# Gradient tiles loaded by GpSimd instead of SP, the first block's leaf C by halves of channels, and a newly planned order in the weight gradient

## Chip, cores and metric

One core of a Trainium2 chip runs one program. The metric is the device time of one execution in microseconds (us); 16 DMA engines serve the core. Engine names are those of the profile: PE (matrix multiplications; PEld its weight loads), DVE (elementwise work on vectors), ACT (activations and copies), POOL (GpSimd; here it clears buffers and issues DMAs), SP (issues DMAs). The memory on the chip is one buffer called arena; ps is the accumulator memory that PE writes.

## What is computed

A strided convolution (31 taps, stride 2, 256 channels to 256), a normalisation over time for each channel, a GELU, and the gradients of all inputs. Two sequences (batch) of 16000 steps, bfloat16:

```
h = sum over i < 31 of einsum('blc,cd->bld', x[:, i:i + 2*L:2], w[i])     # L = 7985
mu  = mean of h over l
var = mean of (h - mu)**2 over l
out = gelu((h - mu) / sqrt(var + 1e-5) * gamma + beta)
outputs: out, then the gradients for x, w, gamma and beta given grad_out
```

## The kernel before

The convolution and its two gradients are split three times in the manner of Karatsuba: two halves A and C_ and a combination B_, so that three products stand for four at each level, at the price of sums and differences on DVE. A bottom product is called a **leaf**. Where a leaf's weights or inputs can be differenced once more, it is computed by `f_three_b` and `f_three_ac` (f for the forward pass) instead of `f_leaf`: one product with a weight difference, three copies on ACT inside ps, and then the outer products onto the copies.

There are five stages. F0 and F1 are the forward pass of the two sequences (matmuls on line 742), G0 and G1 the gradient for x (line 1330), W the gradient for w (line 1537). W goes through nine combinations n = 0 to 8; each takes tiles of x from memory (`x_raw`, `x_more`, 1 MB and 512 KB), tiles of h's gradient (`d_tile`: for each of two sequences one load of 640 KB and one of 576 KB from the scratch memory dld), forms sums of x (lines 1502, 1603, 1607) and differences of d (`pair_d`, lines 1618 and 1623; `leaf_d`, lines 1703 and 1708) on DVE, and multiplies them on PE. The scratch memory dld is written during G0 and G1 by POOL (line 550).

No instruction's place is written by hand. A class `Plan` records each operation with its engine, an assumed duration and what it depends on (`add`); `order` works out when each is due, by going back from the matmuls that need it, and shifts the due time by two tables: `lead` (by the kind of operation) and `fine` (by kind and by n in W). `listing` then lets each engine take, among what is ready, the operation that is due first, and `emit` writes the program in the order that results. On each engine the program then runs strictly in that order. A load goes to SP, except that `load(..., "POOL", own=True)` lets POOL issue it. So a wait of SP for a buffer holds back every DMA behind it on SP; the same goes for POOL.

The start is `f_first` (line 966), the first block of F0. Four ps tiles are used; `pa`, `pc` and `pb` take the leaves A, C_ and B_. Weights are loaded slot by slot by SP (16 loads, most of 256 KB). DVE then makes the weight sums (`w_sub`, line 684): differences W[B][slot] and the second differences WD. DVE's sums of x are line 700; one of them, `third(C_, U[2])`, serves leaf C alone. Three pieces follow in time on PE: leaf A (channel half 0 in two pieces, then half 1), leaf C by `f_three_b` (16 matmuls of 256 columns) and `f_three_ac` (32 of 256), and leaf B in the same way. Line 837 (`keep`) is ACT's reading of leaf B's finished ps tile, the end of this block on PE.

Of the kernel before, what the change touches and what calls it, by code (L numbers as in the profile page):

```python
# [20 lines left out]
A, B_, C_ = 0, 1, 2  # L21
# [17 lines left out]
class Plan:  # L39
# [3 lines left out]
    def __init__(self, tc):  # L43
# [88 lines left out]
            "W keep w_keep": -3.0,  # L132
            "W keep weight_grad": -12.5,
            "W leaf_d weight_grad": 0.5,
            "W load d_tile": -54.0,
            "W load out0_late": 115.0,
            "W load w_done": -7.5,
            "W load w_emit": 28.0,
            "W load weight_grad": 2.0,
            "W load x_more": -9.0,  # L140
            "W load x_raw": 1.0,
            "W pair_d weight_grad": 1.5,
            "W pair_x weight_grad": 1.5,
            "W turn out0_late": -21.0,
            "W ve w_done": -11.0,
            "W ve weight_grad": -25.0,
            "W w_add weight_grad": 2.5,
            "W w_add x_more": 1.5,
            "W w_add x_tile": 29.5,
            "W w_both weight_grad": 11.0,  # L150
            "W w_emit w_done": 13.0,
            "W w_emit weight_grad": -261.0,
            "W w_mm w_leaf": -10.0,
            "W w_pairs weight_grad": -112.5,
        }
        self.spare = {k + " dl_turn": 3.0 for k in ("G0 turn", "G0 load", "G1 turn", "G1 load")}
        self.room, self.mixed = 2048.0, 2.2
# [80 lines left out]
            "W keep w_keep": {0: 2.5, 3: -11.5, 4: 11.0, 5: 6.5, 6: -13.0},  # L238
            "W keep weight_grad": {0: 7.0, 1: 1.5, 2: -4.0, 3: -2.0, 4: 23.5},
            "W leaf_d weight_grad": {0: 1.5, 1: -14.5, 2: -49.5, 3: 27.0, 4: -0.5, 5: -6.5, 6: -16.0, 7: 12.5, 8: -21.0},  # L240
            "W load d_tile": {0: 71.0, 1: 51.0, 2: 44.0, 3: 39.5, 4: 1.0, 5: 4.0, 6: -11.5, 7: 28.0, 8: 93.0},
            "W load out0_late": {0: -80.0, 8: 80.5},
            "W load w_emit": {5: -31.0, 6: -58.5, 7: -34.5, 8: 24.0},
            "W load weight_grad": {7: 81.5},
            "W load x_more": {2: -1.5, 4: 1.0, 5: -17.5},
            "W load x_raw": {0: -0.5, 2: -30.5, 4: 0.5, 5: -92.0, 6: -11.5, 7: 24.0},
            "W pair_d weight_grad": {0: -2.5, 1: -7.5, 2: -34.0, 3: -23.5, 4: 38.0, 5: -129.0, 6: -205.5, 7: -22.0, 8: 4.5},
            "W pair_x weight_grad": {0: 3.0, 1: -23.5, 2: 39.5, 3: -23.0, 4: -14.0, 5: 2.0, 6: -9.5, 7: 27.5, 8: -76.0},
            "W turn out0_late": {0: -66.0, 8: -137.0},
            "W ve w_done": {2: 12.0},  # L250
            "W ve weight_grad": {5: -21.5, 7: 12.0, 8: -47.0},
            "W w_add weight_grad": {0: 16.5, 1: -5.0, 2: 8.5, 3: -0.5, 4: -51.5, 5: -0.5, 6: -28.5, 7: -43.5, 8: 53.0},
            "W w_add x_more": {2: 20.0, 4: 2.0, 5: 34.0},
            "W w_add x_tile": {1: -101.0, 3: -75.5},
            "W w_both weight_grad": {0: -43.0, 1: -23.0, 3: -1.5, 6: -18.0, 7: -12.5, 8: 28.0},
            "W w_emit w_done": {5: -1.5, 6: 5.0, 7: -9.0, 8: -30.5},
            "W w_emit weight_grad": {8: 240.0},
            "W w_mm w_leaf": {2: -7.5, 3: -150.5, 4: 42.5, 5: -233.0, 6: 12.5, 8: 6.0},
            "W w_mm w_pairs": {0: -7.0, 1: 7.0, 2: -47.0, 3: -10.0, 4: -139.5, 5: 2.5, 6: -395.0, 7: 6.0, 8: 14.0},
            "W w_mm w_single": {0: 2.5, 1: 3.5, 2: -9.0, 3: -1.5, 4: -211.5, 5: -4.5, 6: -3.0, 7: 1.5, 8: -24.5},  # L260
            "W w_pairs weight_grad": {0: 25.5, 2: -11.5, 3: 41.5, 4: 15.5, 6: -37.0, 7: -5.0, 8: -17.0},
        }
        self.npe = 0
        self.stage, self.part = "F0", 0
# [206 lines left out]
def conv_stem_kernel(  # L471
# [15 lines left out]
    K, _, D = w.shape  # L487
    P = 128
# [3 lines left out]
    HM = 256  # L492
# [72 lines left out]
    W = {B_: sb(0, 3, 2, 4, 2, D), A: sb(24576, 3, 2, 4, 2, D), C_: sb(49152, 3, 2, 4, 2, D)}  # L565
# [4 lines left out]
    U = [sb(o, 2, F) for o in (138240, 142592, 205312)]  # L570
# [191 lines left out]
    def f_three_b(ps, br, lf, op, co, we):  # L762


        jobs = []
        for dh in range(2):
            for q2 in range(2):
                for par in range(2):
                    for ch in range(2):
                        o0 = (2 * par + ch) * XM + co + q2  # L770
                        n = we if q2 + par + ch else HM
                        jobs.append((0, slice(HM * dh, HM * dh + n), WD[br, lf][:, ch, q2, par, dh * P:(dh + 1) * P],
                                     op[:, 1, o0:o0 + n], dh + q2 + par + ch == 0))
        f_mm(ps, jobs, [ps[:, 0]], [WD[br, lf], op[:, 1]])
        for o, i, sc in ((ps[:, 1, 0:HM], ps[:, 0, HM:512], 1.0), (ps[:, 1, HM:512], ps[:, 0, HM:512], -1.0),
                         (ps[:, 0, HM:512], ps[:, 0, 0:HM], -1.0)):
            add("ACT", act(256), [o], [i],
                lambda o=o, i=i, sc=sc: nc.scalar.activation(out=o, in_=i, func=ACT.Copy, scale=sc))  # L778

    def f_three_ac(ps, br, lf, u, co, we, wo):  # L780
        for half, ua, ww in ((0, u[:, 0], we), (1, u[:, 1], wo)):
            for dh in range(2):
                jobs = []
                for q2 in range(2):
                    for par in range(2):
                        for ch in range(2):
                            q = 2 * q2 + half
                            if i_tap(q, par, br, lf) < K:
                                o0 = (2 * par + ch) * XM + co + q2
                                jobs.append((dh, slice(HM * half, HM * half + ww),  # L790
                                             W[br][:, lf, ch, q, par, dh * P:(dh + 1) * P], ua[:, o0:o0 + ww], False))
                f_mm(ps, jobs, [ps[:, dh]], [W[br][:, lf], ua, ps[:, dh]])
# [1073 lines left out]
```

## Time and profile before

| | |
|---|---|
| device time, median of 3 runs | 1148.43 us (1147.74 to 1150.5) |
| time of the profiled execution | 1148.4 us |
| its span (first to last instruction) | 1146.6 us |
| PE busy | 1117.3 us, 97% |
| DVE busy | 998.8 us, 87% |
| ACT busy | 532.4 us, 46% |
| POOL busy | 124.4 us, 11% |

A row of the timeline shows where a group starts (us from the span's start), how long it takes, its engine, line, operation and tiles, how many there are, and in brackets how long the engine was idle before the group and who ended that idle time ("<-DVE arena L684": a DVE instruction of line 684). A view of windows shows, for each stretch, what each engine was busy and (x) how many instructions it ran, then the granted clock of PE (1.00 is full speed), the mean share of the 16 DMA engines that was busy, and the rate in GB/s. Line numbers of the kernel after are larger by one in every function (742 becomes 743, and so on).

### The profile page before, as it was taken

What the parts mean: (1) busy time and instruction counts of PE and PEld (TensorE: products, weight loads), DVE (VectorE), ACT (ScalarE), POOL (GpSimd) and SP (SyncE); (2) the same over time, 40 slices, a digit from 0 to 9 for tenths busy, and PEclk for the clock granted to TensorE, in tenths of its full rate; (3) what the DMA queues carried; (4) which work ended last, traced back from release to release, by engine and by line L of the source; (5) the groups of instructions that cost most, each with busy time, mean ns of one, the idle gap of its engine ahead of it and who ended that gap; (6) DMA issues with size and microseconds to landing.
All of it is one profiled execution on the core that took longest, in us unless ns stands there. A gap on an engine that the chain in (4) does not pass through costs nothing. (4 is left out here: it accounts for less than half of the span.)

```text
span 1146.6 us, 18837 instructions
## 1 busy us (share of the span) xinstructions
PE 1117.3 (97%) x7598; PEld 749.3 (65%) x7652; DVE 998.8 (87%) x932; ACT 532.4 (46%) x817; POOL 124.4 (11%) x221
## 2 busy tenths in 40 slices
PE   5999999999999999999999899999999999999998
PEld 3888899877777884444444444444488766666785
DVE  7997787798989998998999777976799998788995
ACT  1254453768777488987744255633212212111200
POOL 0000000000000002231233133232200000000000
PEclk8999999999999999999999999999999999999999
DMA  9476658678895699999989688886998815999564
GB/s 220 66 175 138 164 139 172 147 189 192 193 222 132 192 363 277 280 259 277 229 224 218 136 214 190 205 214 163 247 334 267 291 64 200 350 333 308 185 199 128
DMA packets 345999, 243.57 MB, mean 212 GB/s; under 512 B 233569, under 2 KB 317159, under 8 KB 341735
## 3 DMA queue, kind: packets, MB, share of 16 engines
q1 hardware_dynamic: 338807, 223.47, 73.4%
q0 software_dynamic: 7104, 18.89, 5.8%
q8 instruction: 60, 0.98, 0.4%
q14 instruction: 28, 0.23, 0.1%
HBM read 106.24 MB, written 80.25 MB: 163 GB/s over the span
## 5 line engine op out<-in xcount | busy, mean ns | idle before, releaser
L742 PE MATMUL ps<-arena 128*128 128x256 bf16 (+4 forms) x3460 | 408.4, 282 | 12.6 <-DMA arena<-in_x_dram 6.0
L1330 PE MATMUL ps<-arena 128*128 128x512 bf16 (+1 forms) x1833 | 401.6, 377 | 9.5 <-DVE arena L1283 3.3
L742 PEld LDWEIGHTS <-arena 128*128 128x128 bf16 x3460 | 339.1, 99 | 81.7 <-DMA arena<-in_x_dram 6.3
L1330 PEld LDWEIGHTS <-arena 128*128 128x128 bf16 x1872 | 183.6, 98 | 226.3 <-issue 10.2
L1537 PE MATMUL ps<-arena 128*128 128x256 bf16 (+1 forms) x2305 | 308.3, 296 | 3.4 <-DVE arena L1703 1.8
L1537 PEld LDWEIGHTS <-arena 128*128 128x128 bf16 x2320 | 226.7, 98 | 85.1 <-DVE arena L1607 1.9
L837 ACT ACTIVATE arena<-ps 128x1024 f32<-128x1024 f32 x109 | 110.8, 1021 | 253.1 <-PE ps L1537 82.7
L700 DVE TENSOR_TENSOR arena<-arena 128x2080 bf16<-128x2080 bf16 (+8 forms) x126 | 156.5, 1266 | 34.4 <-PE ps L742 33.8
L550 POOL DMA_DIRECT2D dld<-arena x144 | 104.3, 727 | 259.7 <-DMA arena<-arena 247.3
L1117 DVE TENSOR_TENSOR arena<-arena 128x2048 bf16<-128x2048 bf16 (+1 forms) x80 | 95.6, 1195 | 9.1 <-ACT arena L1109 4.9
L1283 DVE TENSOR_TENSOR arena<-arena 128x1032 bf16<-128x1032 bf16 (+1 forms) x126 | 87.4, 725 | 8.1 <-ACT arena L1232 4.8
L1502 DVE TENSOR_TENSOR arena<-arena 128x4096 bf16<-128x4096 bf16 (+1 forms) x50 | 87.1, 1773 | 5.9 <-DMA arena<-in_x_dram 5.7
L1391 DVE TENSOR_TENSOR ps<-ps,arena 128x2048 f32<-128x2048 f32 x30 | 68.9, 2297 | 24.9 <-PE ps L1330 13.8
L1401 DVE TENSOR_TENSOR arena<-ps,arena 128x1024 bf16<-128x1024 f32 x64 | 77.0, 1218 | 8.0 <-PE ps L1330 5.3
L857 ACT ACTIVATE arena<-ps 128x512 bf16<-128x512 f32 (+1 forms) x64 | 37.1, 581 | 54.0 <-PE ps L742 53.5
L1639 ACT COPY ps<-ps 128x256 f32<-128x256 f32 x54 | 19.3, 358 | 84.2 <-PE ps L1537 82.5
L559 POOL MEMSET arena<- 128x128 bf16 (+11 forms) x40 | 8.6, 245 | 428.3 <-DVE arena L700 139.9
L1357 ACT COPY ps<-ps 128x512 f32<-128x512 f32 x48 | 27.7, 577 | 48.6 <-PE ps L1330 48.4
L1708 DVE TENSOR_TENSOR arena<-arena 128x4608 bf16<-128x4608 bf16 x16 | 40.6, 2551 | 4.7 <-PE ps L1537 4.7
L812 ACT ACTIVATE arena<-ps 128x512 f32<-128x512 f32 x56 | 29.6, 597 | 32.3 <-DVE ps L822 18.8
L778 ACT ACTIVATE ps<-ps 128x256 f32<-128x256 f32 x75 | 27.6, 369 | 35.3 <-PE ps L742 34.1
L1623 DVE TENSOR_TENSOR arena<-arena 128x2048 bf16<-128x2048 bf16 x36 | 42.8, 1219 | 1.4 <-PE ps L1537 1.4
(81 smaller groups left out, 716.5 us busy)
## 6 DMA issues: line engine op xcount, KB each, us to landing
arena<-in_x_dram SPq DMA_DIRECT2D x28, 1024.0 KB
dld<-arena POOLq DMA_DIRECT2D x144, 128.0 KB, 4.0
arena<-hd SPq DMA_DIRECT2D x32, 512.0 KB
out_dram<-arena SPq DMA_DIRECT2D x14, 1024.0 KB
arena<-in_x_dram SPq DMA_DIRECT2D x26, 512.0 KB
arena<-dld SPq DMA_DIRECT2D x18, 640.0 KB
arena<-dld SPq DMA_DIRECT2D x18, 576.0 KB
vl<-arena SPq DMA_DIRECT2D x36, 256.0 KB
```

What stands on the lines that cost most here:

```text
L550: lambda: e.dma_start(out=out, in_=in_), dma=np_ * ns / 16e3 * 1.03, ns=ns, tp=SH[pk], slack=slack)
L700: lambda: nc.vector.tensor_tensor(out=o, in0=a, in1=b, op=ALU.add))
L742: yield nc.tensor.matmul(ps[:, dh, cs], lhsT=wt, rhs=mv, start=s0, stop=False, skip_group_check=True)
L837: lambda: nc.scalar.activation(out=out, in_=ps, func=ACT.Copy, scale=scale))
L1117: add("DVE", dve(nf), [o], [a, b_], lambda: V.tensor_tensor(out=o, in0=a, in1=b_, op=op))
L1283: lambda: nc.vector.tensor_tensor(out=o, in0=a, in1=b, op=ALU.subtract))
L1330: yield nc.tensor.matmul(ps[:, e, 0:wide], lhsT=lt, rhs=mv, start=s0, stop=False, skip_group_check=True)
L1391: lambda: nc.vector.tensor_tensor(out=o, in0=x, in1=g, op=ALU.add))
L1401: lambda: nc.vector.tensor_tensor(out=ho[:, :, k, :], in0=ps[:], in1=g, op=ALU.add))
L1502: add("DVE", dve(o.free_size()), [o], [a, b], lambda: nc.vector.tensor_tensor(out=o, in0=a, in1=b, op=ALU.add))
L1537: yield nc.tensor.matmul(ps[:, s, c0:c1], lhsT=lt, rhs=mv, start=s0, stop=False, skip_group_check=True)
L1623: add("DVE", dve(2048), [o], [u, v], lambda o=o, u=u, v=v: nc.vector.tensor_tensor(out=o, in0=u, in1=v, op=ALU.subtract))
```

## The change

Three edits. The rows of the tables `lead` and `fine` for stage W get new numbers, so that the order of W is another one (a few of those rows are shown). In `f_first`, leaf C is computed by `f_leaf` in two pieces, by halves of channels, where it was `f_three_b` with `f_three_ac`; `third(C_, U[2])` goes. And `d_tile` loads from POOL's queue.

```diff
@@ tables of stage W (all its rows change)
-            "W load d_tile": -54.0,
+            "W load d_tile": -66.0,
-            "W pair_d weight_grad": 1.5,
+            "W pair_d weight_grad": -1.0,
...
-            "W pair_d weight_grad": {0: -2.5, 1: -7.5, 2: -34.0, 3: -23.5, 4: 38.0, 5: -129.0, 6: -205.5, 7: -22.0, 8: 4.5},
+            "W pair_d weight_grad": {0: -8.5, 1: -23.0, 2: -53.5, 3: -0.5, 4: 3.5, 5: -1.0, 6: -217.0, 7: 0.5, 8: 19.0},
@@ def f_first(xt)
-        third(C_, U[2])
         third(B_, U[1])
         pa, pc, pb = ring[0], ring[1], ring[3]
         f_leaf(pa, B_, A, ops[A], 0, HM, HM, True, (0,), (0,))
         f_leaf(pa, B_, A, ops[A], 0, HM, HM, False, (0,), (1,))
         f_leaf(pa, B_, A, ops[A], 0, HM, HM, False, (1,))
-        for ps, lf, u in ((pc, C_, U[2]), (pb, B_, U[1])):
-            f_three_b(ps, B_, lf, ops[lf], 0, HM)
-            f_three_ac(ps, B_, lf, u, 0, HM, HM)
+        f_leaf(pc, B_, C_, ops[C_], 0, HM, HM, True, (0,))
+        f_leaf(pc, B_, C_, ops[C_], 0, HM, HM, False, (1,))
+        f_three_b(pb, B_, B_, ops[B_], 0, HM)
+        f_three_ac(pb, B_, B_, U[1], 0, HM, HM)
@@ def d_tile(n, b)
             load(v.rearrange("p r d -> p (r d)"),
-                 bass.AP(tensor=t.tensor, offset=t.offset, ap=[[8 * D, P], [1, k * D]]), k * 65536, 4096)
+                 bass.AP(tensor=t.tensor, offset=t.offset, ap=[[8 * D, P], [1, k * D]]), k * 65536, 4096, "POOL", own=True)
```

What this does to the order is shown at three places. The names in brackets at a row's end are semaphores: DVE_49 counts DVE's finished instructions, DMAHW and DMASW those of DMAs issued by SP and by POOL. Between the first block and the end of G1 the order of PE, DVE and ACT is the same in both programs but for a weight difference that DVE makes later.

PE, at the end of the first half of leaf A (24 matmuls), before:

```order
L742 LDWEIGHTS arena
L742 MATMUL ps<-arena 128x256
L742 LDWEIGHTS arena [waits DVE_49]
L742 MATMUL ps<-arena 128x256 [waits Activation_49]
L742 LDWEIGHTS arena
L742 MATMUL ps<-arena 128x256
```

The same place now, and 48 rows (24 weight loads, 24 matmuls) further on:

```order
L743 LDWEIGHTS arena
L743 MATMUL ps<-arena 128x256
L743 LDWEIGHTS arena [waits DVE_49]
L743 MATMUL ps<-arena 128x512
L743 LDWEIGHTS arena
L743 MATMUL ps<-arena 128x512
```

```order
L743 LDWEIGHTS arena
L743 MATMUL ps<-arena 128x256
L743 LDWEIGHTS arena [waits DVE_49]
L743 MATMUL ps<-arena 128x512 [waits Activation_49]
L743 LDWEIGHTS arena
L743 MATMUL ps<-arena 128x512
```

Before, PE went from leaf A's first half to leaf C's 16 matmuls with the weight differences WD, DVE's sixth `w_sub` of the sixteen that follow on line 684; leaf A's second half came after them. Now leaf A's second half comes at once and waits for DVE's second `w_sub`; then comes leaf C, whose first half waits for the seventh, and leaf B's two pieces come last. On DVE the sixteen `w_sub` stand in another order to suit, with one sum of line 700 less ahead of them; on SP four loads of weights for leaf A's second half stand ahead of leaf C's eight, where they stood behind.

DVE, at the change from G1 (1391, 1401) to W, before:

```order
L1607 TENSOR_TENSOR arena<-arena 128x2048 [waits DVE_49]
L1401 TENSOR_TENSOR arena<-ps,arena 128x2x512 [waits DMAHW2_49,PE_49]
L1618 TENSOR_TENSOR arena<-arena 128x1024 [waits DMAHW7_49,PE_49]
L1618 TENSOR_TENSOR arena<-arena 128x1024 [waits DMAHW3_49]
L1401 TENSOR_TENSOR arena<-ps,arena 128x2x512
L1401 TENSOR_TENSOR arena<-ps,arena 128x2x512 [waits DVE_49,PE_49]
L1401 TENSOR_TENSOR arena<-ps,arena 128x2x512 [waits PE_49]
L1703 TENSOR_TENSOR arena<-arena 128x2304 [waits DMAHW4_49]
L1703 TENSOR_TENSOR arena<-arena 128x2304 [waits DMAHW5_49]
L1618 TENSOR_TENSOR arena<-arena 128x1024 x2
L1703 TENSOR_TENSOR arena<-arena 128x2304
L1623 TENSOR_TENSOR arena<-arena 128x2048 [waits DVE_49,PE_49]
```

and now:

```order
L1608 TENSOR_TENSOR arena<-arena 128x2048 [waits DVE_49]
L1402 TENSOR_TENSOR arena<-ps,arena 128x2x512 [waits DMAHW7_49,PE_49]
L1402 TENSOR_TENSOR arena<-ps,arena 128x2x512 [waits PE_49]
L1402 TENSOR_TENSOR arena<-ps,arena 128x2x512 [waits DVE_49,PE_49]
L1402 TENSOR_TENSOR arena<-ps,arena 128x2x512 [waits PE_49]
L1608 TENSOR_TENSOR arena<-arena 128x2048 [waits DVE_49] x2
L1619 TENSOR_TENSOR arena<-arena 128x1024 [waits DMASW3_49]
L1619 TENSOR_TENSOR arena<-arena 128x1024 [waits DMASW4_49]
L1619 TENSOR_TENSOR arena<-arena 128x1024 x2
L1704 TENSOR_TENSOR arena<-arena 128x2304 [waits DMASW5_49]
L1704 TENSOR_TENSOR arena<-arena 128x2304
```

The four small differences of `pair_d` (1618, now 1619) stand behind the four of line 1402 and behind two sums of x (1608); two of them stood between the former. On PE, the first 8 matmuls of W now stand behind the last of G1 (they stood ahead of its last 4); 24 more of W follow, and the next one needs the first 1619.

SP, in combination n = 1 and 2 of W, before, with the d tiles dld among the x tiles:

```order
L550 DMA arena<-in_x_dram 128x4x512
L550 DMA arena<-dld_1_81 128x2560
L550 DMA arena<-dld_1_90 128x2560
L550 DMA arena<-in_x_dram 128x4x512
L550 DMA arena<-dld_1_81 128x2304
L550 DMA arena<-dld_1_90 128x2304
L550 DMA arena<-in_x_dram 128x4x512
L550 DMA arena<-in_x_dram 128x8x512 x3
```

SP there now, and behind it POOL where its stores to dld end:

```order
L551 DMA out_dram<-arena 1024x1x256 x4
L551 DMA arena<-in_x_dram 128x4x512 x4
L551 DMA arena<-in_x_dram 128x8x512 x4
L551 DMA arena<-in_x_dram 128x4x512 x4
L551 DMA pcd_98<-arena 128x1024
```

```order
L551 DMA dld_4_93<-arena 128x2x256 x2
L551 DMA arena<-dld_0_80 128x2304
L551 DMA arena<-dld_0_89 128x2304
L551 DMA arena<-dld_0_80 128x2560
L551 DMA arena<-dld_0_89 128x2560
L551 DMA dld_7_96<-arena 128x2x256 x2
L551 DMA arena<-dld_2_82 128x2560
L551 DMA arena<-dld_2_91 128x2560
```

All 36 loads of d tiles have left SP; on POOL four of them stand ahead of the last two stores of dld, and the other 32 follow one another, with nothing but a small store behind them.

More of the change, by code (lines that the diff above doesn't have):

```diff
@@ L131, in __init__ @@
             "G1 zero e_comp": -8.0,
-            "W keep w_keep": -3.0,
-            "W keep weight_grad": -12.5,
-            "W leaf_d weight_grad": 0.5,
-            "W load d_tile": -54.0,
[L136 to L141, printed above, removed]
-            "W pair_d weight_grad": 1.5,
+            "W keep w_keep": -1.0,
+            "W keep weight_grad": -73.0,
+            "W leaf_d weight_grad": -5.5,
+            "W load d_tile": -66.0,
+            "W load out0_late": 45.0,
+            "W load w_done": -6.0,
+            "W load w_emit": 41.5,
+            "W load weight_grad": 97.5,
+            "W load x_more": -8.5,
+            "W load x_raw": 2.0,
+            "W pair_d weight_grad": -1.0,
             "W pair_x weight_grad": 1.5,
-            "W turn out0_late": -21.0,
-            "W ve w_done": -11.0,
-            "W ve weight_grad": -25.0,
+            "W turn out0_late": -103.0,
+            "W ve w_done": -7.0,
+            "W ve weight_grad": -18.0,
             "W w_add weight_grad": 2.5,
[L148 to L154, printed above, removed]
+            "W w_add x_tile": -39.0,
+            "W w_both weight_grad": 11.5,
+            "W w_emit w_done": 12.0,
+            "W w_emit weight_grad": -291.5,
+            "W w_mm w_leaf": -13.5,
+            "W w_mm w_pairs": -0.5,
+            "W w_pairs weight_grad": -125.0,
         }
@@ L237, in __init__ @@
             "G1 zero e_comp": {2: 20.0, 3: 23.0},
[L238 to L243, printed above, removed]
@@ new lines, in __init__ @@
+            "W keep weight_grad": {0: 14.0, 1: 68.0, 2: 4.0, 3: -18.0, 4: 3.5},
+            "W leaf_d weight_grad": {0: -10.5, 1: 24.5, 2: -54.0, 3: 14.5, 4: 20.5, 5: 27.0, 7: 33.5, 8: -21.0},
+            "W load d_tile": {0: 63.0, 1: 10.0, 2: 27.0, 3: 76.5, 4: -1.0, 5: -10.0, 6: 7.5, 7: -27.0, 8: 96.0},
+            "W load out0_late": {0: -50.0, 8: 220.5},
+            "W load w_done": {3: -0.5},
+            "W load w_emit": {5: -54.0, 6: -73.5, 7: -47.5, 8: 9.0},
+            "W load weight_grad": {7: -53.0},
@@ new lines, in __init__ @@
+            "W load x_more": {2: -9.5, 4: 2.0, 5: -17.5},
+            "W load x_raw": {0: -0.5, 2: -3.5, 4: -0.5, 5: -119.5, 6: -14.0, 7: 6.5},
+            "W pair_d weight_grad": {0: -8.5, 1: -23.0, 2: -53.5, 3: -0.5, 4: 3.5, 5: -1.0, 6: -217.0, 7: 0.5, 8: 19.0},
+            "W pair_x weight_grad": {0: 4.5, 1: 4.0, 2: 39.5, 3: -19.0, 4: -11.0, 5: -7.5, 6: -12.0, 7: 27.0, 8: -35.0},
+            "W turn out0_late": {8: -124.0},
+            "W ve w_done": {2: 10.5},
+            "W ve weight_grad": {5: 37.5, 6: -31.0, 7: 15.0, 8: -10.5},
@@ L262, in __init__ @@
+            "W w_mm w_pairs": {0: -8.5, 1: -223.0, 2: -142.5, 3: -5.0, 4: -227.5, 5: 10.0, 6: -259.0, 7: 6.0, 8: 14.0},
+            "W w_mm w_single": {0: 2.5, 1: 3.5, 2: -0.5, 3: -1.5, 4: -196.0, 5: -37.0, 6: -4.0, 7: 2.5, 8: -84.5},
+            "W w_pairs weight_grad": {0: 1.5, 1: 3.0, 2: -8.5, 3: -11.5, 4: 10.0, 5: 13.5, 6: -5.5, 7: -23.0, 8: -9.0},
         }
```

25 lines of the change are left out of this document (8 added, 17 removed).

## Prediction

> **What bounds the kernel.** I read the page first, then PE's timeline at the start and in W, then DVE's and ACT's beside it, and last the windows for the clock and the DMA engines.
>
> ```profile
> span 1146.6 us, 18837 instructions
> PE 1117.3 (97%) x7598; PEld 749.3 (65%) x7652; DVE 998.8 (87%) x932; ACT 532.4 (46%) x817; POOL 124.4 (11%) x221
> ```
>
> PE is busy for 1117.3 of 1146.6 us, so what can be won is the 29.3 us in which it is idle, and time in which its clock is low. The change touches two places: the first 40 us and the stage W, from about 825 us on. Here is PE at the start, then DVE and ACT.
>
> ```profile
> 12.21 6.44 PE L742 MATMUL ps<-arena 128*128 128x512 bf16 x24 [1.88 <-DVE arena L700]
> 23.07 37.15 PE L742 MATMUL ps<-arena 128*128 128x256 bf16 x307 [4.42 <-DVE arena L684]
> ...
> 12.67 3.53 DVE L700 TENSOR_TENSOR arena<-arena 128x2080 bf16<-128x2080 bf16 x3
> 16.12 18.24 DVE L684 TENSOR_TENSOR arena<-arena 128x2048 bf16<-128x2048 bf16 x16
> 34.28 2.33 DVE L700 TENSOR_TENSOR arena<-arena 128x4192 bf16<-128x4192 bf16 x1
> ...
> 33.64 1.17 ACT L778 ACTIVATE ps<-ps 128x256 f32<-128x256 f32 x3 [5.71 <-PE ps L742]
> 39.77 1.03 ACT L837 ACTIVATE arena<-ps 128x1024 f32<-128x1024 f32 x1 [4.96 <-PE ps L742]
> ```
>
> PE ends leaf A's first half at 12.21 + 6.44 = 18.65 and stands until 23.07. Leaf C's matmuls wait for the sixth of the sixteen weight differences: 16.12 + 6 x 1.14 (18.24 / 16) = 22.96. ACT's line 837 waits for PE and starts at 39.77, so the first block ends on PE at about 39.65. From 23.07 to 60.22 PE has no wait.
>
> ```profile
> 20.00:22.00 2.00, 0.00 (x0) 0.00 (x0) 2.00 (x3) 0.00 (x0) 0.00 (x0) 0.84 1.31 140
> 22.00:24.00 2.00, 0.93 (x5) 0.69 (x6) 2.00 (x2) 0.00 (x0) 0.00 (x0) 0.50 1.05 236
> ...
> 26.00:28.00 2.00, 2.00 (x10) 1.09 (x8) 2.00 (x3) 1.10 (x3) 0.00 (x0) 0.50 0.36 76
> 28.00:30.00 2.00, 2.00 (x17) 1.55 (x16) 2.00 (x3) 0.00 (x0) 0.00 (x0) 0.95 0.00 0
> ...
> 32.00:36.00 4.00, 4.00 (x35) 3.18 (x34) 4.00 (x4) 1.10 (x3) 0.00 (x0) 1.00 0.00 0
> 36.00:40.00 4.00, 4.00 (x39) 3.57 (x37) 4.00 (x5) 0.23 (x1) 0.00 (x0) 1.00 0.00 0
> ```
>
> The wait costs twice. The granted clock is 0.50 until about 28.2 (0.95 from 28 to 30 us is 0.2 us at half), so from 23.07 on some 5.13 us run at half speed: 10 matmuls in 2 us against 74 in 8 us at full clock, 0.108 us each. Half of 5.13, 2.56 us, is lost to the clock.
>
> **The start, step by step.** The times of the new order by these rows:
> - DVE has one sum of line 700 less (3.53 / 3, with overlap 1.15 us), so the sixteen differences start at 14.97. Leaf A's first half is untouched and ends at 18.65. Its second half needs the second difference, at 14.97 + 2.28 = 17.25, and runs on without a wait: 24 matmuls with the columns of 32 matmuls of 256, at 0.108 us 3.46 us, to 22.11.
> - Leaf C's first half needs the seventh, at 14.97 + 7.98 = 22.95, and starts at 23.05 (0.1 us from DVE to PE, as 22.96 to 23.07): PE stands 0.94 us. Leaf C's two halves are 64 times 256 columns, 6.91 us, to 29.96. Before, they were 48 such: 16 x 0.108 = 1.73 us is added.
> - Leaf B follows: 16 matmuls, 1.73 us, to 31.69. Then the outer products wait for two of ACT's three copies, 2 x 0.39 (1.17 / 3) and two hand-overs of 0.13: 1.04 us. Before, leaf A's second half stood in this place and hid the copies. 32 more matmuls: 32.73 + 3.46 = 36.19.
>
> Against 39.65 that is 3.46 us earlier; put together from the differences it is -(4.42 - 0.94 - 1.04) - 2.56 + 1.73 = -3.27. After that PE meets DVE, which is only 1.15 us earlier: the sum at 34.28 now ends at about 35.4, a difference of line 684 at 36.5, then three of line 700 at 37.7, 38.8 and 40.0. PE needs the first of these after 16 further matmuls, at 37.9, the next at 39.6: it fits by 0.2 us. I take **-3.0 us**, with 0.3 us for PE waiting on DVE there, and as ends -3.5 (no wait) and -1.15 (DVE sets the pace). Three ACT copies fewer (1.17 us) are worth nothing, since ACT stood idle 5.71 us before such a group. The four weight loads that move ahead of leaf C's put those back by some 3.6 us at most (1 MB at 290 GB/s), but the sixteen end when they did; the DMA row of 20 to 22 us has fallen to 140 GB/s, so the last landed by about 21, and the seventh difference starts at 21.81.
>
> The two new waits, 0.94 and 1.04 us, must not bring the low clock back. Rows on that:
>
> ```profile
> 659.79 40.45 PE L1330 MATMUL ps<-arena 128*128 128x512 bf16 x176 [3.28 <-DVE arena L1283]
> 650.00:700.00 50.00, 46.45 (x206) 20.82 (x210) 39.75 (x38) 26.11 (x34) 13.81 (x23) 0.97 0.88 197
> 800.00:850.00 50.00, 47.78 (x294) 28.75 (x296) 42.62 (x33) 11.94 (x17) 7.24 (x10) 1.00 0.99 291
> ```
>
> An idle stretch of 3.28 us at 656.5 lowered the mean clock of 50 us to 0.97 (1.5 us lost, about 3 us at half); one of 1.79 us at 842.75 (below) left it at 1.00. In the start it fell at about 21.36 (0.84 in that window), 2.7 us into the wait. So about 1 us is safe. [...]
>
> **W.** PE and DVE at the change from G1 to W:
>
> ```profile
> 830.41 1.04 PE L1537 MATMUL ps<-arena 128*128 128x256 bf16 x8
> 831.29 1.03 PE L1330 MATMUL ps<-arena 128*128 128x512 bf16 x4
> 832.15 9.77 PE L1537 MATMUL ps<-arena 128*128 128x256 bf16 x88
> 842.14 0.61 PE L1537 MATMUL ps<-arena 128*128 128x256 bf16 x4 [0.22 <-DVE arena L1607]
> 844.54 52.76 PE L1537 MATMUL ps<-arena 128*128 128x256 bf16 x480 [1.79 <-DVE arena L1703]
> 897.65 3.23 PE L1537 MATMUL ps<-arena 128*128 128x256 bf16 x28 [0.35 <-DVE arena L1607]
> 901.06 9.10 PE L1537 MATMUL ps<-arena 128*128 128x256 bf16 x72 [0.18 <-DVE arena L1623]
> ...
> 827.30 1.22 DVE L1607 TENSOR_TENSOR arena<-arena 128x2048 bf16<-128x2048 bf16 x1
> 829.57 1.33 DVE L1618 TENSOR_TENSOR arena<-arena 128x1024 bf16<-128x1024 bf16 x2
> 830.81 3.48 DVE L1401 TENSOR_TENSOR arena<-ps,arena 128x1024 bf16<-128x1024 f32 x3
> 843.14 1.35 DVE L1703 TENSOR_TENSOR arena<-arena 128x2304 bf16<-128x2304 bf16 x1
> 873.04 2.28 DVE L1603 TENSOR_TENSOR arena<-arena 128x4096 bf16<-128x4096 bf16 x1
> ```
>
> PE's waits in W up to 910 us are 0.22 + 1.79 + 0.35 + 0.18 = 2.54 us, all on DVE. DVE works without a stop there, so a new order can move these waits, but each product put forward puts another back. The times below are in before's clock; the 3.0 us shift both engines alike.
> - The first 1619. On DVE: from 827.30 one 1608, four 1402 and two 1608 at 1.13 us from start to start, 7.9 us, then 0.69 (two take 1.33): 835.9. On PE: G1's last four matmuls end 8 matmuls earlier, about 831.4; then 32 of W at 0.111 (9.77 / 88), to 834.95. PE waits about **1.0** us, in place of the 1.79, which go: the four 1704 are ready at 842.8, and PE gets to the third of them, 64 matmuls later, at 843.1. I take 1.3, since the last of G1 may be later; ends 0 and 1.8. A 1624 and a 1608 behind them fit to within 0.4 us: +0.4.
> - The 1604 (1603 before). PE asks for it 64 matmuls earlier in its order, 7.1 us. DVE brings it 6.3 us earlier: five of line 1623 (1.13 each) that stood ahead of it now stand behind, and a wait of 0.43 us for a d tile goes. Before, it was ready 0.6 us ahead of PE (285 matmuls of 0.110 after 844.54 is 875.9, against 873.04 + 2.28 = 875.32), so now PE waits 0.2 or, with PE no longer held by the 1.79, up to 1.5: +1.0.
>
> That gives 1.3 + 0.4 + 1.0 = 2.7 against 2.54: **+0.2 us**, ends -2.5 (no wait is left) and +2.
>
> The move of the loads:
>
> ```profile
> SPq L550 <- DVE arena L1708: 38.5, 4, 28.7
> L550 SPq DMA_DIRECT2D arena<-dld x32: 338/498/4787, 828.9 to 1086.9; - x32
> L550 POOL DMA_DIRECT2D dld<-arena x144: 726/726/773, 449.2 to 826.6; - x144
> DVE arena L1502 <- DMA arena<-in_x_dram: 5.7, 3, 5.3
> sum 45.00, PE 44.84 PEld 28.08 DVE 40.67 ACT 7.26 POOL 0.00; mean PE 4.98 PEld 3.12 DVE 4.52 ACT 0.81 POOL 0.00
> 1000.00:1005.00 5.00, 5.00 (x48) 4.50 (x46) 4.97 (x4) 1.07 (x3) 0.00 (x0) 1.00 1.10 352
> arena<-dld SPq DMA_DIRECT2D x18, 640.0 KB
> arena<-dld SPq DMA_DIRECT2D x18, 576.0 KB
> ```
>
> SP loses 36 issues of about 0.5 us (32 of them in W), of no worth as it waits most of the time; POOL gains 36, taken at 0.73 us like its stores, 26 us in a stretch in which it does nothing (0.00 in the sum). What changes is the queue: SP stood up to 28.7 us at a d load whose buffer line 1708 still read, with x loads behind it. Now x loads go past. That is worth little, since PE never waited for a DMA in W, and DVE only 5.7 us for x. On the other side the d loads now run beside x loads. Between 985 and 1030 us the DMA engines are full (about 350 GB/s), and DVE is busy 40.67 of 45. The four d tiles of one n are 2432 KB, 7.1 us at that rate; an x tile delayed by all of it uses up DVE's 4.3 us of slack and holds PE for 2.8. I take half for the one place, **+1.3 us**; ends 0 and 5.6 (two places in full). [...]
>
> **Sum.** -3.0 + 0.2 + 1.3 = -1.5 us. The profiled execution took 1148.4 us (span 1146.6 and 1.8 around it), the median is 1148.43: **1146.9 us**. A measurement of this kernel tells about 0.3%, 3.4 us, from no change, so this counts as no change.
>
> **Rivals.**
> - The loads are not what they seem: no DMA term at all, as PE never waited for one. -3.0 + 0.2 gives 1145.6, still within 0.3%. For it: PE is busy 44.84 of 45 us in the fullest stretch. Against: full DMA engines. 0.20.
> - W's waits vanish as well: -3.0 - 2.5 gives 1142.9, and half of that with no DMA term 1144.4. Against it stands DVE without a stop from 825 to 907. 0.28.
> - DVE sets the start: -1.15 in place of -3.0, 1148.8. For it: DVE's products fit by 0.2 us only. 0.10.
> - Slower: d loads in POOL's queue, no longer placed among the x loads, go ahead of x tiles that DVE is waiting for. It decides from 4.3 us of delay on. Each place costs up to 2.8; at three of the six combinations from n = 3 on it is 8.4: -3.0 + 0.2 + 8.4 gives 1154.0. 0.12.
> - My forecast: 0.30.
>
> Faster by over 0.3% is the second rival, 0.28; slower the fourth, 0.12; the rest, 0.60, is within. The range runs from 1143.0 (nearly all of the second rival) to 1150.8 (the start by DVE, with +3.5 in W), and leaves out the fourth.
>
> **What would show it.** In PE's timeline the 4.42 us before 23 us are gone, with a wait of about 1 us near 22 and one near 31.7, a clock of 1.00 from 18 on, and line 838 of ACT at about 36.3. G1's end, and the first matmul of W, come 3 us earlier. In W there is a wait on 1619 in place of the one on 1703, and one on 1604. Wrong would be: a clock of 0.50 after 22 us; less than 2 us gained when W begins; or waits of DVE for in_x_dram of over 4 us between 980 and 1100.

## The result, and the profile after

The changed kernel took 1155.78 us (median of 4 runs, 1153.75 to 1156.55) against 1148.13 us of the kernel before beside it: a ratio of 1.0066, 95% interval 1.0048 to 1.0084. It is slower by 7.6 us, outside the range forecast (1143.0 to 1150.8). A second comparison (six runs, on another occasion) gave 1155.55 us and 1.0064 (1.0046 to 1.0082). The profile is of the fastest of the first four: 1153.75 us, span 1151.9.

The rows of the kernel after that answer to those of before, its page first:

```profile
span 1151.9 us, 18895 instructions
PE 1121.6 (97%) x7652; PEld 748.6 (65%) x7652; DVE 997.5 (87%) x931; ACT 531.0 (46%) x814; POOL 143.5 (12%) x257
```

PE's timeline at the start:

```profile
11.97 9.45 PE L743 MATMUL ps<-arena 128*128 128x512 bf16 x48 [1.88 <-DVE arena L701]
22.90 8.90 PE L743 MATMUL ps<-arena 128*128 128x512 bf16 x64 [1.48 <-DVE arena L685]
32.72 67.54 PE L743 MATMUL ps<-arena 128*128 128x256 bf16 x612 [0.92 <-ACT ps L779]
```

a window of 2 us there:

```profile
22.00:24.00 2.00, 1.10 (x8) 0.70 (x8) 2.00 (x3) 0.00 (x0) 0.00 (x0) 1.00 0.93 198
```

ACT's timeline, at its reading of leaf B's result:

```profile
36.42 1.02 ACT L838 ACTIVATE arena<-ps 128x1024 f32<-128x1024 f32 x1 [3.35 <-PE ps L743]
```

and DVE's, at the sixteen weight differences:

```profile
14.74 18.32 DVE L685 TENSOR_TENSOR arena<-arena 128x2048 bf16<-128x2048 bf16 x16
```

The differences start at 14.74 (14.97 was forecast), and the wait of 4.42 us is gone. Two waits of 1.48 and 0.92 us stand in its place, the granted clock stays at 1.00 behind them, and ACT reads leaf B's result at 36.42, where it was 39.77: 3.35 us earlier. After that PE runs to 100 us without a wait.

W is where the time went. PE's timeline in W:

```profile
826.84 3.61 PE L1331 MATMUL ps<-arena 128*128 128x512 bf16 x16 [0.72 <-DVE ps L1392]
830.29 3.66 PE L1538 MATMUL ps<-arena 128*128 128x256 bf16 x32
835.37 10.65 PE L1538 MATMUL ps<-arena 128*128 128x256 bf16 x96 [1.42 <-DVE arena L1619]
848.46 22.80 PE L1538 MATMUL ps<-arena 128*128 128x256 bf16 x192 [2.43 <-DVE arena L1608]
871.80 134.46 PE L1538 MATMUL ps<-arena 128*128 128x256 bf16 x980 [0.55 <-DVE arena L1604]
1008.18 4.98 PE L1538 MATMUL ps<-arena 128*128 128x256 bf16 x44 [1.92 <-DVE arena L1608]
1014.26 134.03 PE L1538 MATMUL ps<-arena 128*128 128x256 bf16 x976 [1.10 <-ACT arena L838]
```

From the first matmul of W to the last it is 318.0 us (830.29 to 1014.26 + 134.03 = 1148.29). Before, it was 312.3 us (830.41 to 1142.74), with 0.9 us of G1's last matmuls among them: W is 6.6 us longer. PE's waits add up to 7.42 us, against 2.54. The first matmul of W came 0.12 us earlier in this execution (830.29 against 830.41) and not 3; where the start's gain went is taken up at the decisive pair below. The 1.42 and 0.55 were foreseen; the 2.43 at 846 to 848.5 and the 1.92 and 1.10 at 1006 to 1014 were not. DVE's timeline names what ended the waits behind them:

```profile
844.91 1.22 DVE L1624 TENSOR_TENSOR arena<-arena 128x2048 bf16<-128x2048 bf16 x1 [2.71 <-DMA out_dram<-arena]
985.68 1.23 DVE L1503 TENSOR_TENSOR arena<-arena 128x2048 bf16<-128x2048 bf16 x1 [3.66 <-DMA arena<-in_x_dram]
992.22 1.23 DVE L1503 TENSOR_TENSOR arena<-arena 128x2048 bf16<-128x2048 bf16 x1 [3.04 <-DMA arena<-in_x_dram]
```

Three windows of 2 us show the clock behind the first:

```profile
848.00:850.00 2.00, 1.54 (x13) 1.30 (x14) 2.00 (x3) 0.00 (x0) 0.00 (x0) 0.90 1.05 336
850.00:852.00 2.00, 2.00 (x11) 1.40 (x10) 2.00 (x3) 0.00 (x0) 0.00 (x0) 0.50 1.34 334
852.00:854.00 2.00, 2.00 (x16) 1.57 (x15) 2.00 (x3) 0.00 (x0) 0.00 (x0) 0.75 1.35 188
```

and the waits of DVE in W (us in total, times, longest) sum up those for x tiles:

```profile
DVE arena L1503 <- DMA arena<-in_x_dram: 8.8, 5, 3.7
```

Line 1624 writes a buffer of which the last store of the gradient for x still reads, and stands 2.71 us for it; PE then waits 2.43 us and runs at half clock for 3.4 us more (0.4, 2.0 and 1.0 us of the three windows, by their 0.90, 0.50 and 0.75), another 1.7 us. Near 985 and 992 DVE waits for x tiles. So in both places a DMA of SP's queue is late. What ran beside it? The transfers between 982 and 993 us, by queue (packets, MB, share of the 16 engines' time; software_dynamic is what POOL issued):

```profile
q0 software_dynamic: 576, 2.49, 56.0%
q1 hardware_dynamic: 1808, 1.85, 48.4%
```

and the same between 985 and 991 us, while both queues have work throughout:

```profile
q0 software_dynamic: 455, 2.01, 82.4%
q1 hardware_dynamic: 446, 0.44, 20.9%
```

POOL's timeline there:

```profile
980.14 2.09 POOL L551 DMA_DIRECT2D arena<-dld  x4 [34.99 <-DVE arena L1709]
```

SP's:

```profile
977.64 44.75 SPq L551 DMA_DIRECT2D arena<-in_x_dram  x18
```

And a row of the chain of waits that ended last (start, us, what):

```profile
985.06 10.35 DMA arena<-in_x_dram
```

The four d tiles of n = 5 are issued at 980.14, as soon as line 1709 has freed their buffers, and take 56% of the engines' time between 982 and 993. That mean hides how the two queues share: from 985 to 991 as many packets, as the profile counts them, go from the one as from the other (455 and 446), and as POOL's are 4.4 KB on average (2.01 MB / 455) and SP's 1.0 KB, POOL's take four fifths of the time. The x tiles, which DVE is waiting for, get a fifth; in the chain one issued at 985.06 needs 10.35 us, after which DVE's and PE's work up to 1014 hangs on it. At the store it is the same: between 836 and 840 us 303 packets of POOL's took 79.0% and 305 of SP's 23.5%.

### The profile page after: what moved, and what is told of

Its sections match the earlier page's. It is cut to its first block, busy times and chain, and to the rows that moved or that the text cites. A ratio compares the mean times of both kernels' runs of the same rounds, so it can differ in the third digit from the quotient of the medians.

```text
span 1151.9 us, 18895 instructions
## 1 busy us (share of the span) xinstructions
PE 1121.6 (97%) x7652; PEld 748.6 (65%) x7652; DVE 997.5 (87%) x931; ACT 531.0 (46%) x814; POOL 143.5 (12%) x257
## 5 line engine op out<-in xcount | busy, mean ns | idle before, releaser
L1331 PE MATMUL ps<-arena 128*128 128x512 bf16 x1872 | 404.2, 378 | 8.8 <-DVE arena L1284 3.2
L701 DVE TENSOR_TENSOR arena<-arena 128x2064 bf16<-128x2064 bf16 (+8 forms) x125 | 155.4, 1267 | 31.6 <-PE ps L743 31.1
L551 POOL DMA_DIRECT2D arena<-dld x36 | 19.0, 532 | 255.4 <-DVE arena L1709 207.0
L1358 ACT COPY ps<-ps 128x512 f32<-128x512 f32 x48 | 27.7, 578 | 48.5 <-PE ps L1331 48.4
```

What stands on the lines that cost most here:

```text
L551: lambda: e.dma_start(out=out, in_=in_), dma=np_ * ns / 16e3 * 1.03, ns=ns, tp=SH[pk], slack=slack)
L701: lambda: nc.vector.tensor_tensor(out=o, in0=a, in1=b, op=ALU.add))
L1331: yield nc.tensor.matmul(ps[:, e, 0:wide], lhsT=lt, rhs=mv, start=s0, stop=False, skip_group_check=True)
```

## The experiments

Theories at the outset. **Queue**: the d tiles, once in POOL's queue, take the DMA engines from x tiles and from the store, which are needed sooner. **Order**: the new tables make DVE ask too early for a buffer or a tile, whoever loads d. **Start**: the first block is worth 3 us by itself, and keeps them.

The kernels are compared by their ratio to the kernel before beside them; W is PE's time from the first to the last matmul of W in the profiled execution, "waits" the sum of PE's waits in it; where the order of W is that of before, 0.9 us of G1's matmuls lie in it too.

| kernel | median us (runs) | ratio, 95% interval | W us | waits us |
|---|---|---|---|---|
| changed kernel again | 1155.55 (6) | 1.0064 (1.0046 to 1.0082) | 321.2 | 8.7 |
| start alone | 1146.03 (12) | 0.9983 (0.9968 to 0.9998) | 312.7 | 2.5 |
| start alone, again | 1145.91 (11) | 0.9981 (0.9969 to 0.9993) | | |
| POOL and tables | 1157.64 (6) | 1.0083 (1.0062 to 1.0104) | 320.2 | 8.0 |
| start and tables, d planned on SP | 1170.83 (5) | 1.0200 (1.0174 to 1.0226) | | |
| POOL alone, planned again | 1188.65 (6) | 1.0374 (1.0340 to 1.0408) | | |
| changed order, SP issues | 1146.76 (12) | 0.9990 (0.9977 to 1.0003) | 314.1 | 5.2 |
| order of before, POOL issues | 1158.13 (6) | 1.0083 (1.0061 to 1.0106) | 323.1 | 9.6 |
| no d tiles for n = 1 | 1149.22 (10) | 1.0008 (0.9993 to 1.0023) | 316.0 | 5.3 |
| no d tiles for n = 5 | 1151.01 (10) | 1.0025 (1.0008 to 1.0042) | 317.3 | 6.2 |
| n = 1 and 5 by SP | 1148.66 (12) | 1.0010 (0.9995 to 1.0025) | 313.9 | 4.7 |
| n = 1 and 5 held up on POOL | 1151.24 (11) | 1.0022 (1.0009 to 1.0035) | 319.7 | 9.2 |

**The parts alone.** The start in the kernel before (e1_start), and the changed kernel without it (e6_pool_tables); the diff is that of the first block, forwards or backwards.

> The kernel before with only the edit of the first block (leaf C by f_leaf in two halves); tables and queues of before, so the order of W is that of before. Start theory (the start is worth 3.0 us by itself, and is kept to the end): 1145.1 us, 0.997 to 0.998 of before; the 4.42 us of PE's waiting before leaf C are replaced by two waits of 1.5 and 0.9 us, W begins 3 us earlier and is as long as before. Rival (the shift of the start is eaten on the way, since transfers in G and at the change to W meet other work): W begins only 1 to 2 us earlier, 1146.5 to 1147.5 us.

> The changed kernel with the first block of before: d tiles from POOL and the new tables alone. Start theory: 3 us slower than the changed kernel, 1158 to 1159 us, with W as long as in the changed kernel (318 us against 312 before). Rival (W's loss comes from meeting the earlier work at the change from G1 to W, that is from the shift): W is as long as before, 1148 to 1150 us.

PE's timeline of the start alone, and its first matmuls of W:

```profile
23.12 8.90 PE L742 MATMUL ps<-arena 128*128 128x512 bf16 x64 [1.93 <-DVE arena L684]
825.20 1.04 PE L1537 MATMUL ps<-arena 128*128 128x256 bf16 x8
```

The start theory holds: 1146.03 us, and W as long as before (312.7 against 312.3). The ratios 0.9983 and, repeated, 0.9981 are 2.0 and 2.2 us, with 3 us inside both intervals; without the start the changed kernel is at 1.0083 in place of 1.0066, again 2 us, though there the intervals overlap. W begins 5.2 us earlier in that execution, more than the start gives, in part since a low clock near 660 us did not occur in it (its mean granted clock is 1.000, and 176 matmuls there took 38.84 us; before they took 40.45, and the clock from 650 to 700 us was 0.97); single executions of one kernel differ there (below). So the loss lies in POOL and the tables together.

> The kernel before with the new first block alone, once more, since its first interval ended close to 1: if the start is worth 2 to 3 us, 1145 to 1146.5 us and a ratio of 0.997 to 0.999 whose interval stays under 1; if the first comparison was luck, a ratio of 0.999 to 1.001.

**The two other parts, planned again.** The d tiles back on SP in the changed kernel, and on POOL in the kernel before, with the plan left to follow:

```diff
-  ..., k * 65536, 4096, "POOL", own=True)     # e4_sp: the changed kernel
+  ..., k * 65536, 4096)
-  ..., k * 65536, 4096)                       # e2_pool: the kernel before
+  ..., k * 65536, 4096, "POOL", own=True)
```

> The changed kernel with the d tiles loaded by SP again; new tables and new start stay. Queue theory (d tiles in POOL's queue take the DMA engines from x tiles and from the last store of the gradient for x, so these land late): most of W's loss goes, the time is 1146 to 1149 us, and no x tile between 975 and 995 us takes over 10 us from issue to landing. Order theory (the new order lets line 1624 write a buffer that a store still reads, whoever loads d): the wait of 2.4 us in PE near 847 us stays, with the low clock behind it, 1151 to 1154 us.

> The kernel before with only the d tiles moved to POOL (the order of W is planned again by the old tables). Queue theory: slower than before by 3 us or more, 1151 to 1156 us, with PE or DVE waiting for x tiles or stores in W. Order theory: the move alone is worth little, 1147 to 1150 us.

Both came out far beyond either theory, at 1170.83 and 1188.65 us. One row of PE's timeline for each, the longest wait in W:

```profile
1013.01 51.26 PE L1538 MATMUL ps<-arena 128*128 128x256 bf16 x317 [6.51 <-DVE arena L1624]
```

```profile
1050.97 53.85 PE L1537 MATMUL ps<-arena 128*128 128x256 bf16 x345 [11.37 <-DVE arena L1607]
```

These runs do not tell the theories apart: the planner makes another order for every engine (in the second even in G0 and G1), with tables that were set for the other queue. What follows is that one must not let the plan move when the queue is the question.

**Only the issuing engine.** The plan is kept, and with it the order on PE, DVE and ACT; only the engine that issues a d tile is changed, at the place that the plan gave it.

```diff
-    e = {"SP": nc.sync, "POOL": nc.gpsimd, "ACT": nc.scalar}[eng]
+    e = {"SP": nc.sync, "POOL": nc.gpsimd, "ACT": nc.scalar}[by or eng]
-    ..., k * 65536, 4096, "POOL", own=True)           # x1_same_sp: the changed kernel
+    ..., k * 65536, 4096, "POOL", own=True, by="SP")
-    ..., k * 65536, 4096)                             # x2_same_pool: the kernel before
+    ..., k * 65536, 4096, by="POOL")
```

> The changed kernel, planned as it is (PE, DVE, ACT in the same order), but the d tiles are issued by SP, at the places among SP's DMAs that the plan gave them on POOL. Queue theory (two queues that run side by side make x tiles and the store land late): the x tile issued near 978 us lands by 988 in place of 992, DVE's waits for in_x_dram fall from 8.8 to under 4 us, and the time is 1150 to 1153 us. Rival (one queue or two, the same bytes compete; what is late is late through the places in the order): 1154 to 1158 us, with the waits near 847 and 1008 us as they are. A d load that waits for its buffer would hold back x tiles behind it on SP; if that decides, it is over 1158 us.

> The kernel before, planned as it is, but POOL issues the d tiles: the same order on PE, DVE and ACT, and on SP without the d tiles. Queue theory: x tiles land later where d tiles now go beside them, DVE waits over 8 us for in_x_dram in W, 1151 to 1155 us. Rival (the queue alone is worth nothing): 1147 to 1149.5 us, DVE's waits for x at most the 5.7 us of before.

PE's timeline of the changed order with SP issuing:

```profile
831.30 12.40 PE L1538 MATMUL ps<-arena 128*128 128x256 bf16 x112 [1.42 <-DVE arena L1619]
843.86 19.37 PE L1538 MATMUL ps<-arena 128*128 128x256 bf16 x176 [0.17 <-DVE ps L1648]
864.47 134.03 PE L1538 MATMUL ps<-arena 128*128 128x256 bf16 x968 [1.23 <-DVE arena L1604]
1000.13 5.40 PE L1538 MATMUL ps<-arena 128*128 128x256 bf16 x48 [1.63 <-DMA arena<-dld]
1006.29 134.03 PE L1538 MATMUL ps<-arena 128*128 128x256 bf16 x969 [0.76 <-DVE arena L1624]
```

SP's timeline there, at the x tiles and d tiles of the place that is late with POOL:

```profile
972.31 0.34 SPq L551 DMA_DIRECT2D arena<-dld  x1
974.23 11.30 SPq L551 DMA_DIRECT2D arena<-in_x_dram  x6
985.59 0.97 SPq L551 DMA_DIRECT2D arena<-dld  x2
988.63 1.52 SPq L551 DMA_DIRECT2D arena<-in_x_dram  x2
990.20 2.51 SPq L551 DMA_DIRECT2D arena<-dld  x1
```

PE's timeline of the order of before with POOL issuing, the longest wait:

```profile
1009.98 142.32 PE L1537 MATMUL ps<-arena 128*128 128x256 bf16 x1029 [5.25 <-DVE arena L1607]
```

and DVE's waits for x tiles in W (us in total, times, longest):

```profile
DVE arena L1502 <- DMA arena<-in_x_dram: 12.5, 3, 12.0
```

This is the decisive pair. The changed order with SP issuing takes 1146.76 us: 8.8 us less than with POOL (8.5 by the ratios). The order of before with POOL issuing takes 1158.13 us, 9.8 us more than with SP (9.5 by the ratio). The queue costs about 9 to 10 us whichever order stands round it. The wait of 2.43 us behind the store is gone with SP (line 1624 no longer waits; the 0.17 at that place is for another line); three of the four d tiles of n = 5 stand behind six or more x tiles, and DVE's waits for x tiles in W are 5.1 us in place of 8.8 (under 4 was expected). In the second kernel DVE waits 12.0 us at one x tile, and PE 5.25. My expectations had the sign of the queue theory and too small a size: 1150 to 1153 and 1151 to 1155. The order by itself is worth nothing that shows: start with the new order (0.9990, 0.9977 to 1.0003) against start with the old one (0.9981, 0.9969 to 0.9993), whose intervals overlap.

One trace alone does not give the size. The profiled executions of the changed order with POOL and with SP are 7.7 us apart (1153.75 and 1146.03), of which W makes 3.9 (318.0 and 314.1); 3.7 us are there by 756 us already, before the first d tile is loaded (817 us), and so are not the queue's. In the other pair they are 9.3 us apart (1157.73 and 1148.4), and W alone 10.8 (323.1 and 312.3).

**Which d tiles.** In the changed kernel POOL clears the buffers of one n in place of loading them, all else the same; these kernels leave out that part of the gradient for w.

```diff
-    lambda: e.dma_start(out=out, in_=in_), dma=...
+    lambda: e.memset(out, 0.0) if clear else e.dma_start(out=out, in_=in_), dma=...
-    ..., k * 65536, 4096, "POOL", own=True)
+    ..., k * 65536, 4096, "POOL", own=True, clear=n == 1)   # x5_clear5: n == 5
```

> The changed kernel with the four d tiles of the second combination (n = 1, those issued near 831 us) not loaded: POOL clears the buffers instead (this part of the weight gradient is left out); every order stays. Queue theory: without these 2.4 MB the last store of the gradient for x lands before 841 us, line 1624 does not wait for it, PE's wait of 2.43 us near 847 us and the low clock behind it are gone, W is 3 to 4 us shorter than the 318 us of the changed kernel, 1151 to 1153 us. Order theory (the store is simply asked for too early): PE still waits 1.5 us or more there.

> The changed kernel with the four d tiles of n = 5 (issued near 980 us) not loaded, cleared by POOL instead (that part of the weight gradient is left out). Queue theory: the x tiles behind 978 us land within 8 us, DVE's waits for in_x_dram between 980 and 996 us (7.5 us) fall under 2, PE's waits of 1.92 and 1.10 us near 1008 and 1014 us go, the time is 1152 to 1154 us. Rival (x tiles are late by their own bytes and buffers): these waits stay.

PE's timeline without the d tiles of n = 1, and then without those of n = 5, at the places of the late waits:

```profile
844.65 19.37 PE L1538 MATMUL ps<-arena 128*128 128x256 bf16 x176 [0.16 <-DVE ps L1648]
1002.17 140.82 PE L1538 MATMUL ps<-arena 128*128 128x256 bf16 x1013 [2.46 <-DVE arena L1608]
```

```profile
847.93 23.68 PE L1538 MATMUL ps<-arena 128*128 128x256 bf16 x192 [4.21 <-DVE arena L1608]
872.15 273.12 PE L1538 MATMUL ps<-arena 128*128 128x256 bf16 x1985 [0.54 <-DVE arena L1604]
```

Each clears its own place and leaves the other: without n = 1 the wait at the store is 0.16 us and that near 1002 is still 2.46; without n = 5 there is no wait from 872 to the end, and 4.21 us at the store. The times fall by 6.3 and 4.5 us from 1155.55, more than expected (1151 to 1153, 1152 to 1154). The order theory, by which the store is simply asked for too early, is out.

**Two places by SP, and two held up.** First the d tiles of n = 1 and 5 alone by SP at their planned places (`by="SP" if n in (1, 5) else None`); then all by POOL, with 28 clearings of a small tile ahead of the four of n = 1 and of the last three of n = 5:

```diff
+        def go():
+            for _ in range(late):
+                yield nc.gpsimd.memset(zt2, 0.0)
+            yield e.dma_start(out=out, in_=in_)
```

> The changed kernel once more, beside the next two on one chip, since four runs are few: 1154 to 1157 us, mean granted clock 0.996 or less.

> The changed kernel, same plan and order, with the d tiles of n = 1 and n = 5 alone issued by SP at their planned places, the other 28 by POOL. If the two places found in the trace (the store near 845 us, the x tiles near 980 to 996 us) hold the whole cost of the queue, 1147 to 1149 us; if the cost is spread over all combinations, 1150 to 1153 us.

> The changed kernel with POOL issuing all d tiles, but held up by 28 clearings of a small buffer (6 to 9 us) ahead of the four of n = 1 and ahead of the last three of n = 5. If the cost is that d tiles not yet needed go beside x tiles and a store that are, the store lands before 842 us and the x tiles issued near 978 us before 989 us, and the time is 1147 to 1151 us. If two queues cost by themselves, whenever the loads are issued, it stays at 1154 to 1157 us.

With two places by SP 1148.66 us: 6.9 of the 8.8 us are in those eight loads, as expected (1147 to 1149). The remaining 1.9 would be the other 28's, but the intervals of that kernel and of the one with SP issuing all overlap. The delay gains 4.3 us, to 1151.24, just beyond its range; it came out longer than planned (10.3 us for 28 clearings, where 6 to 9 were expected). PE's timeline there, two rows of the chain that ended last, and DVE's sum of waits for x tiles (line 1508 is line 1503 of the changed kernel, 1611 is 1604, 1615 is 1608):

```profile
842.72 19.37 PE L1545 MATMUL ps<-arena 128*128 128x256 bf16 x176 [0.16 <-DVE ps L1655]
865.82 136.13 PE L1545 MATMUL ps<-arena 128*128 128x256 bf16 x972 [3.73 <-DVE arena L1611]
1004.69 4.98 PE L1545 MATMUL ps<-arena 128*128 128x256 bf16 x44 [2.74 <-DVE arena L1615]
```

```profile
837.35 16.62 DMA arena<-in_x_dram
988.16 10.63 DMA arena<-in_x_dram
```

```profile
DVE arena L1508 <- DMA arena<-in_x_dram: 11.9, 8, 4.7
```

The store is in time again (its line no longer waits), so the second queue cost nothing at that store once the d tiles went later; but the held-up tiles, issued from 836.54 and from 986.59, now meet the next x tiles, which need 16.62 and 10.63 us, and the 0.55 us at 871 has become 3.73. W's waits are 9.2 us in that execution, as many as with POOL at once. Moving the collision is not removing it.

## Why the prediction was wrong

The sum was -3.0 (start) + 0.2 (order of W) + 1.3 (queue) = -1.5 us. Measured: about -2 for the start, nothing that shows for the order, and +9 to +10 for the queue.

- **Start: right.** The steps put ACT's line 838 at 36.19 + 0.1; it came at 36.42. The two waits were to be 0.94 and 1.04 us; they are 1.48 (PE came to leaf C at 21.42 and not at 22.11: it started 0.24 us earlier, and its 48 matmuls took 9.45 us where I had 9.90) and 0.92 (two copies 0.77 and both hand-overs together 0.15 us; the 0.13 for each hand-over was my estimate, without a row). The clock stayed at 1.00 behind both, as forecast. In the time it is 2.0 and 2.2 us, with -3.0 within both intervals (0.9968 and 0.9969 are -3.6 us).
- **The first 1619, the 1704 and the 1604: right in kind.** 1.3 us was taken for the first; it is 1.42, with POOL and with SP issuing. The wait on 1703 is gone. The 1604 was to cost 1.0 and costs 0.55 (1.23 with SP issuing).
- **The step that failed first: "A 1624 and a 1608 behind them fit to within 0.4 us".** I added up DVE's durations and did not ask what else the 1624 waits for. It waits for a store of SP's queue to let go of its buffer, and stood 2.71 us for it (4.21 us of PE's time where only n = 5 was cleared). In the kernel before, the same store cost nothing, and in the new order with SP issuing it cost nothing either: the fit held as a matter of order, and it is the queue that broke it, which the sum had priced at another place alone. That wait for a buffer still being read counted like the 3.66 and 3.04 us of DVE's waits for x tiles.
- **The step that failed most: "I take half for the one place, +1.3 us; ends 0 and 5.6".** The rate of 350 GB/s was right, and so, nearly, was the price of a place in full: 2.8 us, where PE's waits at 1008 and 1014 are 1.92 + 1.10 = 3.02. Two things were wrong. The half was a guess without a row: the x tiles had 20.9% of the engines' time between 985 and 991 us and moved 0.44 MB, which is 1.3 us at 350 GB/s, so by an estimate they lost 4.7 of these 6 us. And I counted only a stretch in which x tiles were dense; the place at 830 to 845 us was shown as full too (0.99 in the row from 800 to 850), and I left it out, with the clock that it brings down. The whole cost is 9 to 10 us, beyond the end of 5.6.
- **The clock.** I asked only whether the start's waits would bring the low clock, not whether W's would. Of the 3.9 us by which W is longer with POOL than with SP issuing in the profiled executions, PE's waits make 2.2 (7.4 against 5.2) and the half clock the other 1.7; in the second execution of the changed kernel W is 7.1 us longer, of which waits make 3.5 (8.7 against 5.2), and the rest, 3.6, is put down to the clock. Over whole executions the mean granted clocks (0.9951 over ten runs, times 1155; 0.9985 over twelve) give at most 5.7 us lost against 1.7, an estimate: a low clock while PE stands costs nothing, and part of it lies before W.
- **The rival "slower"** had the mechanism: "d loads in POOL's queue, no longer placed among the x loads, go ahead of x tiles that DVE is waiting for". It got 0.12, as I read "PE never waited for a DMA in W" as evidence that DMAs do not matter there. It was the result of the order on one queue. With that order kept and only the queue changed, DVE waits 12.0 us at one x tile. Its 8.4 us, from three places at 2.8, came near the measured size; that is partly luck, as two places held most of it and the clock was not in it. The sign that it would show, waits of DVE for in_x_dram of over 4 us between 980 and 1100, came: 3.66 + 3.04 + 0.51 + 0.26 = 7.47 us by 996.

Why the bytes, which are the same, hurt more in two queues: the transfers from 976 to 1000 us in the kernel before, and in the changed kernel.

```profile
DMA packets 6212, 8.50 MB, mean 354 GB/s; under 512 B 232, under 2 KB 5571, under 8 KB 6211
```

```profile
DMA packets 6253, 8.55 MB, mean 356 GB/s; under 512 B 224, under 2 KB 5612, under 8 KB 6252
```

Nothing is lost in rate: 8.50 and 8.55 MB. What changes is who is served first. On SP's queue the d tiles stand among the x tiles at planned places, and in this stretch behind the x tiles that DVE needs next. On POOL they go as soon as a buffer is free, some 28 us ahead of the 1709 that needs them (980.14 and 1008.04), and take four fifths of the engines' time until they are through. While both queues have work, the trace shows one packet for one: 455 and 446 between 985 and 991 us. With 4.4 KB a packet on one side and 1.0 KB on the other the turn is even in packets and not in time (82.4% and 20.9%). The low end of my term for the move was 0; the two kernels in which only the issuing engine was changed give 9 to 10 us.

What stays open: whether the other 28 d tiles cost anything (1.9 us between the medians), and why the time before W differs between executions of one kernel.

The version to keep is the start alone, on the kernel before: 0.9983 and 0.9981, 2 us better than before and 9.5 better than the changed kernel.

## What to carry to other kernels

The order on SP's queue was a priority list here: with the changed order, DVE waited 5.1 us for x tiles when SP issued the d tiles at planned places among them, and 8.8 us when POOL issued them. Loads that need not be early belong behind those that must be, and moving them to another queue, to let them go "for free", let them take turns packet by packet here, which with packets of 4.4 KB against 1.0 KB was four fifths of the DMA engines' time. Where DMA engines are full (354 to 356 GB/s between 976 and 1000 us here), price such a move at what the urgent queue then loses, at every place, and look through the waits of each moved instruction for stores that still read its buffer. And to test a queue in a planned kernel, change only the engine that issues, with the plan held: planning again (1170.8 and 1188.7 us) hid an effect of 9 us under others.

## What was not expected of the hardware

- In the changed kernel two queues that both had work took turns packet by packet: 455 packets of POOL's and 446 of SP's between 985 and 991 us, 303 and 305 between 836 and 840, 295 and 320 between 1092 and 1096. So the queue with the big packets (4.3 to 4.4 KB on average against 1.0 to 1.1 KB) had 77.5% to 82.4% of the engines' time. Over a longer window, in which POOL's tiles start late and end early, the shares look even (56.0% and 48.4% from 982 to 993).
- POOL's issue of a load of 576 or 640 KB took 0.53 us (2.09 us for four), less than the 0.73 us of its 128 KB stores.
- Behind a wait of 2.43 us the clock was at half (0.50 from 850 to 852 us), while behind one of 3.17 us near 655 us in the start alone it did not fall (a mean granted clock of 1.000 over that execution; 176 matmuls in 38.84 us, against 40.45 behind 3.28 us in the kernel before). It was at half for 3.4 us behind the 2.43 and for 6.8 at the start of the kernel before (21.36 to 28.2 us). Behind the wait of 2.13 us near 1013 in the second execution of the changed kernel the clock is 0.84 from 1012 to 1016 and 0.73 from 1016 to 1020, and behind the 1.92 near 1008 in the first it stays at 1.00. The length of a wait alone did not tell which one brings it.
- Before W, executions of one kernel differ by some us with the same order: the first matmul of W came at 830.29 us in one execution of the changed kernel and at 833.11 in another:

```profile
833.11 3.66 PE L1538 MATMUL ps<-arena 128*128 128x256 bf16 x32
```
